# Attention and two MLPs on one core: the start of ScalarE, a later load and eight low halves moved

## The chip, the cores and the metric

The kernel runs on one core of a Trainium2 chip. A core has TensorE (PE: matrix products, with its weight loads PEld), VectorE (DVE), ScalarE (ACT), GpSimd (POOL) and SyncE (SP); SyncE and GpSimd issue the DMAs here, each from a queue that is worked off in order. The metric is the time on the device from the first to the last instruction, in microseconds; less is better.

## The reference

Four batches of 768 steps and eight heads of 48 go through an attention with complex decays, then through a block that mixes tokens and channels, then through a channel MLP behind a layer norm.

```python
def _attn_ref(q, k, v, a_re, a_im):
    mag = np.sqrt(a_re * a_re + a_im * a_im)
    scale = np.minimum(mag, 0.999) / (mag + 1e-06)
    a_re_n, a_im_n = (a_re * scale, a_im * scale)
    for t in range(S):
        ar, ai = (a_re_n[:, :, t, :, None], a_im_n[:, :, t, :, None])
        new_re = ar * S_re - ai * S_im
        new_im = ar * S_im + ai * S_re
        kv = np.einsum('bhd,bhe->bhde', k[:, :, t], v[:, :, t])
        S_re, S_im = (new_re + kv, new_im)
        y[:, :, t] = np.einsum('bhd,bhde->bhe', q[:, :, t], S_re)

def _moe_ref(x, w_tok1, w_tok2, w_ch1, w_ch2):
    h = np.maximum(x.transpose(0, 2, 1) @ w_tok1, 0.0) @ w_tok2
    u = x + h.transpose(0, 2, 1)
    return u + np.maximum(u @ w_ch1, 0.0) @ w_ch2

def _moe2_ref(x, g_ln, w_ch1, w_ch2):
    mu = np.mean(x, axis=-1, keepdims=True)
    var = np.mean((x - mu) ** 2, axis=-1, keepdims=True)
    xn = (x - mu) / np.sqrt(var + 1e-06) * g_ln
    return x + np.maximum(xn @ w_ch1, 0.0) @ w_ch2
```

## The kernel before

The recurrence is turned into matrix products over chunks of 128 steps: with the running product of the normalised decays at hand, the rows of q and k of a chunk are multiplied and divided by it (the corrections), and a head is then a handful of 32-bit matmuls. The decays of a batch come as three pieces of 128 rows, each in two halves of 384 columns. The program is written as four generators whose steps a driver records in turn, and a scheduler sets each engine's order from that recording:

- `gen_E` works on VectorE through a helper (all of its VectorE instructions have line L179). `gen_A` normalises a half piece: ScalarE squares (L228), takes a logarithm (L232), an exponential (L233) and a square with a running sum (L234), and VectorE joins them with four instructions of 384 columns and one of 768; then come the scan steps, each two products `p<-aj` and two sums `aj<-p`. `gen_L2` finishes the scan over blocks. `gen_C` applies the corrections to a half piece and stores it into the tiles of the heads by DMA, the part for k by L355 and the part for q and k by L356 (`stk`, or for the first batch's later heads tiles named `w`). For batch 0 the pieces 0 and 1 go first, then piece 2 (`PARTS`). `load_a` (L63) loads decays of a batch and a piece; `load_qk` (L151) loads q and k.
- `gen_P` does the heads on TensorE: transposes (L425), scores (L438), states (L465), output (L485, L497), with the mask (L443) and the state scan (L466) on VectorE, and the loads of v (L376) on SyncE.
- `gen_W` prepares the weights. A weight comes as raw 64-bit numbers (L513); VectorE unpacks it (L530, L531) to 32 bits, ScalarE rounds it, scaled, to 16 bits (L533, the high half), VectorE subtracts that from the scaled weight (L534, the low half). Weights 0 to 3 are those of the token layers, 4 to 15 those of the first channel MLP, 16 to 27 those of the second.
- `gen_M` does the MLPs with three 16-bit matmuls for each product (high times high, high times low, low times high: L566, L567, L568): the first token layer in two halves (`tok1_half`, result L608 and L610), the second (`tok2`, L612 to L627), the channel MLP (`mlp`, hidden layer by L574 on ScalarE and L576 on VectorE), and the layer norm (`gen_LN`, column sums by 32-bit matmuls L680 and L699 with the constant `ones`).

TensorE accumulates in eight PSUM banks: two under the tag m1, three under m2, one each under sc, tr and y. The second accumulation of the first batch's MLP, which runs five steps behind the first, uses sc, tr and y. The first batch's pass is the one in which everything is prepared; the three batches after it run with all weights in place, and the heads of a later batch are recorded among the MLP steps of the batch ahead.

## Time and profile before

| | us |
|---|---|
| median of 3 runs (lowest to highest) | 973.39 (971.98 to 974.5) |
| the profiled execution, its own time | 972.28 |
| its span, first to last instruction | 970.6 |
| TensorE busy | 834.6 (86%) |
| VectorE busy | 744.1 (77%) |
| ScalarE busy | 496.8 (51%) |
| mean granted TensorE clock | 0.957 |

The busy times are sums over stages that differ: a share of 86% says nothing of the stage in which an engine waits. The rows that follow the change are read by stage. A row of a timeline gives start, length, engine, line, operation, destination and source, and in brackets how long the engine sat idle before it and what released it; where instructions overlap in the pipeline, the distance of two starts is the time that one holds its engine.

### The profile page before, as it was taken

To read this page: it belongs to the slowest core of one execution; us is meant where nothing else is said; L and a number is where in the kernel's file an instruction comes from. 1 tells how busy PE (TensorE), PEld (TensorE's weight loads), DVE (VectorE), ACT (ScalarE), POOL (GpSimd) and SP (SyncE) were. 2 spreads that over 40 slices of the span, in tenths; PEclk is the share of its full clock that TensorE was granted. 3 is DMA by queue.
4 is the path that set the end of the run, shared out by engine and by line. 5 is a ranking of instruction groups with operands and counts; after the bars stand their busy time and mean duration, and the time that the engine had idled before them with its cause. 6 is when DMAs were issued, how large, how long until landed. Compare 5 with 4: busy or idle time off the path is not lost.

```text
span 970.6 us, 15833 instructions
## 1 busy us (share of the span) xinstructions
PE 834.6 (86%) x5738; PEld 570.6 (59%) x5738; DVE 744.1 (77%) x1597; ACT 496.8 (51%) x1364; POOL 59.6 (6%) x113
## 2 busy tenths in 40 slices
PE   0018989699988899999889999799999999999996
PEld 0018979356556687655556666466666666656563
DVE  6999957999997788997979999988675523264543
ACT  6014434533543459434868972574676533354532
POOL 0000101000102100001010000011000000011110
PEclk9999975799999789999899999999999999999998
DMA  8024475421447533114245120343120102255572
GB/s 283 0 57 128 160 208 164 167 79 66 153 133 225 159 107 107 64 34 130 57 118 168 32 62 1 115 127 80 55 56 25 50 1 90 86 194 195 190 239 94
DMA packets 45287, 108.28 MB, mean 112 GB/s; under 512 B 5904, under 2 KB 28560, under 8 KB 45200
## 3 DMA queue, kind: packets, MB, share of 16 engines
q1 hardware_dynamic: 36816, 61.57, 21.5%
q0 software_dynamic: 8384, 45.62, 14.2%
q8 instruction: 47, 0.77, 0.3%
q14 instruction: 40, 0.33, 0.1%
HBM read 77.20 MB, written 11.01 MB: 91 GB/s over the span
## 4 chain that ended last, share of the span: by engine, by line
PE 40%; DVE 28%; DMA 11%; issue 10%; ACT 6%; SPq 4%; POOL 0%; DVEq 0%; POOLq 0%; ACTq 0%
PE m L566 11%; PE m L567 11%; PE m L568 11%; DVE t L179 6%; DVE aj L179 4%; DVE p L179 4%; DMA stk<-t 3%; DMA stk<-qk 2%; DMA raw<-in_wm 2%; DMA aj<-in_a 2%; DVE hid L576 2%; PE sc L438 2%; SPq L355 2%; SPq L356 1%; DVE qk L179 1%
## 5 line engine op out<-in xcount | busy, mean ns | idle before, releaser
L576 DVE SCALAR_TENSOR_TENSOR hid<-m,hid 128x384 f16<-128x384 f32 x198 | 109.4, 553 | 113.4 <-ACT hid L574 112.8
L566 PE MATMUL m<-u,w 128*128 128x384 f16 x576 | 189.6, 330 | 1.5 <-DVE u L626 1.3
L567 PE MATMUL m<-u,w 128*128 128x384 f16 x576 | 189.8, 330 | 0.0
L568 PE MATMUL m<-u,w 128*128 128x384 f16 x576 | 189.7, 329 | 0.0
L574 ACT ACTIVATE hid<-m 128x384 f16<-128x384 f32 x198 | 96.0, 485 | 180.8 <-PE m L568 179.7
L567 PE MATMUL m<-hid,w 128*128 128x384 f16 x540 | 177.3, 329 | 12.3 <-DVE hid L576 12.0
L568 PE MATMUL m<-hid,w 128*128 128x384 f16 x540 | 177.0, 328 | 0.0
L568 PEld LDWEIGHTS <-w 128*128 128x128 f16 x1176 | 116.5, 99 | 89.7 <-issue 20.8
L567 PEld LDWEIGHTS <-w 128*128 128x128 f16 x1176 | 116.9, 99 | 75.1 <-issue 6.5
L566 PEld LDWEIGHTS <-w 128*128 128x128 f16 x1176 | 116.7, 100 | 75.2 <-issue 7.6
L566 PE MATMUL m<-hid,w 128*128 128x384 f16 x540 | 129.6, 328 | 2.4 <-ACT hid L574 2.1
L425 PE MATMUL tr<-cst,stk 96*128 96x96 f32 x125 | 17.1, 260 | 77.8 <-DMA stk<-qk 75.0
L179 DVE SCALAR_TENSOR_TENSOR t<-t 128x384 f32<-128x384 f32 x120 | 64.8, 549 | 8.5 <-ACT t L228 5.7
L425 PEld LDWEIGHTS tr<-cst,stk 96*128 96x128 f32 x125 | 13.9, 151 | 81.4 <-issue 71.3
L179 DVE TENSOR_TENSOR p<-aj 128x288 f32<-128x288 f32 (+2 forms) x150 | 52.7, 392 | 0.8
L179 DVE TENSOR_TENSOR t<-aj,I 128x768 f32<-128x768 f32 x40 | 36.4, 953 | 16.5 <-DMA stk<-t 11.8
L438 PE MATMUL sc<-stk 96*128 96x128 f32 x300 | 46.2, 289 | 2.7 <-DVE xc L682 1.4
L438 PEld LDWEIGHTS sc<-stk 96*128 96x128 f32 x300 | 42.3, 202 | 5.8 <-DVE r L443 1.7
L533 ACT ACTIVATE w<-raw 128x768 f16<-128x768 f32 x28 | 25.4, 906 | 30.0 <-DVE raw L531 29.8
L513 POOL DMA_DIRECT2D raw<-in_wm x48 | 25.9, 540 | 238.3 <-DVE w L534 109.0
L574 ACT ACTIVATION_READ_ACCUMULATOR hid<-m 128x1 f32 x198 | 38.5, 194 | 0.0
L546 ACT ACTIVATE sq<-sq 128x768 f16<-128x768 uint8 x28 | 23.6, 843 | 27.8 <-DVE sq L545 27.8
(268 smaller groups left out, 1670.7 us busy)
## 6 DMA issues: line engine op xcount, KB each, us to landing
raw<-in_wm POOLq DMA_DIRECT2D x48, 768.0 KB, 4.6
qk<-in_qk SPq DMA_DIRECT2D x23, 384.0 KB, 4.7
aj<-in_a SPq DMA_DIRECT2D x9, 768.0 KB, 5.0
stk<-t SPq DMA_DIRECT2D x40, 144.6 KB, 3.3
stk<-qk SPq DMA_DIRECT2D x40, 144.6 KB, 3.1
raw<-in_wt SPq DMA_DIRECT2D x6, 768.0 KB, 5.4
v<-in_v SPq DMA_DIRECT2D x32, 144.0 KB, 2.2
x_d<-xc SPq DMA_DIRECT2D x24, 192.0 KB, 2.5
```

Of the source, the lines that this page charges most:

```text
L179: r = getattr(nc.vector, n)(*a, **k)
L355: nc.sync.dma_start(out=stk[b, h][d0:d0 + m, hf], in_=R[r:r + m])
L425: T.transpose(tr[:, c * 96:(c + 1) * 96], qc(c, 1), eye[0:96, 0:96])
L438: last = T.matmul(sc[:, (c % 3) * P:(c % 3 + 1) * P], qc(c, 1), qc(c, 0), start=True, stop=True)
L513: (nc.sync if n < NSY else nc.gpsimd).dma_start(out=raw.bitcast(U8), in_=w_src[n].bitcast(U8)[:, 3:3 + 8 * S])
L533: wact[n] = A.activation(out=dst[:, :, 0], in_=w, func=AF.Copy, scale=WS).ins
L546: A.activation(out=t[:, HB:2 * HB].bitcast(F16), in_=bad_, func=AF.Copy, accum_out=wstat[:, n:n + 1])
L566: T.matmul(out_, wh, xh_, start=first, stop=False)
L567: T.matmul(out_, wh, xl_, start=False, stop=False)
L568: T.matmul(out_, wl, xh_, start=False, stop=last)
L574: A.activation(out=hl[:, 0], in_=p, func=AF.Relu, accum_out=hstat[:, n_h[0]:n_h[0] + 1])
L576: last[:] = [V.scalar_tensor_tensor(out=hl[:, 1], in0=p, scalar=0.0, in1=hl[:, 0], op0=ALU.max, op1=ALU.subtract).ins]
```

## The change

It has four parts. ScalarE's first instruction on a half piece of batch 0 is held back until the sum of the half piece ahead is done, and the square of the layer norm's gains (`gstat`) goes from VectorE to ScalarE. The decays of batch 1 are loaded when all corrections of batch 0 are recorded, not each after its own piece. For the weights 4 to 11 the low half is formed by TensorE: the 32-bit weight times a scaled identity (`eye_w`) minus the high half times a 16-bit identity (`eye_m`), accumulated in the bank y, for each of its two halves of 384 columns, and ScalarE copies the result out. The first token layer's halves accumulate in tr instead of y, and heads with an even number take m1 instead of tr for the transposes.

```diff
--- before.py
+++ after.py
@@ -96,7 +96,6 @@
     V.memset(bias[:, 5:6], TINY)
     b_ln, b_one, b_eps, b_zero, b_eps_s, b_tiny = (bias[:, i:i + 1] for i in range(6))
     A.activation(out=eye_h, in_=eye, func=AF.Copy, scale=WS * WS)
-    V.tensor_tensor(out=gstat, in0=gl, in1=gl, op=ALU.mult)
 
     w1 = ap.tile([P, FT, 4 * DM], F16, name="w1")
     w1_f = w1.rearrange("p k s -> p (k s)").bitcast(F32)
@@ -210,9 +209,12 @@
                 for i in part:
                     for x in gen_C(b, i, Ct, st, nxt_q):
                         yield x
-                    if b + 1 < B:
+                    if b and b + 1 < B:
                         load_a(b + 1, i)
                     yield ("done", b, i)
+                if b == 0 and part[-1] == 2:
+                    for i in range(3):
+                        load_a(1, i)
 
     av = aj.rearrange("p x (j k r) -> p x j k r", j=6, k=KB)
 
@@ -225,14 +227,15 @@
                 ah = steps(aj, i, hf)
                 t = scratch(b, 2 * i + hf)
                 s4, s5, s6, s7 = (t[:, j * HB:(j + 1) * HB] for j in range(4))
-                A.activation(out=t[:, 0:2 * HB].rearrange("p (x h s) -> p x h s", x=2, h=2), in_=ah, func=AF.Square)
+                with (tc.issue_after(fin["ln"]) if b == 0 and "ln" in fin else ExitStack()):
+                    A.activation(out=t[:, 0:2 * HB].rearrange("p (x h s) -> p x h s", x=2, h=2), in_=ah, func=AF.Square)
                 yield "wait"
                 V.scalar_tensor_tensor(out=s4, in0=s4, scalar=TINY, in1=s5, op0=ALU.add, op1=ALU.add)
                 nn = s4
                 A.activation(out=s5, in_=nn, func=AF.Ln)
                 A.activation(out=s5, in_=s5, func=AF.Exp, scale=-0.5, bias=b_ln)
-                A.activation(out=s6, in_=s5, func=AF.Square, scale=1.0 / 0.4995,
-                             accum_out=rstat[:, 6 * b + 2 * i + hf:6 * b + 2 * i + hf + 1])
+                fin["ln"] = A.activation(out=s6, in_=s5, func=AF.Square, scale=1.0 / 0.4995,
+                                         accum_out=rstat[:, 6 * b + 2 * i + hf:6 * b + 2 * i + hf + 1]).ins
                 if b == 0:
                     V.tensor_scalar(out=s7, in0=s5, scalar1=-EPS / 0.4995, scalar2=1.0, op0=ALU.mult, op1=ALU.add)
                 else:
@@ -531,8 +534,21 @@
         V.scalar_tensor_tensor(out=y.bitcast(U32), in0=y.bitcast(U32), scalar=5, in1=pad[0], op0=ALU.logical_shift_right, op1=ALU.bitwise_or)
         w = y.bitcast(F32).rearrange("p (i s) -> p i s", i=2)
         wact[n] = A.activation(out=dst[:, :, 0], in_=w, func=AF.Copy, scale=WS).ins
+        if NW0 <= n < NW1:
+            if not eye_w:
+                eye_w.append(ap.tile([P, P], F32, name="eye_w"))
+                eye_w.append(ap.tile([P, P], F16, name="eye_m"))
+                A.activation(out=eye_w[0], in_=eye, func=AF.Copy, scale=WS)
+                A.activation(out=eye_w[1], in_=eye, func=AF.Copy, scale=-1.0)
+            for i in range(2):
+                p = psum("y", 1)[:, 0:HB]
+                T.matmul(p, eye_w[0], w[:, i], start=True, stop=False)
+                T.matmul(p, eye_w[1], dst[:, i, 0], start=False, stop=True)
+                A.activation(out=dst[:, i, 1], in_=p, func=AF.Copy)
+            return
         wop[n] = V.scalar_tensor_tensor(out=dst[:, :, 1], in0=w, scalar=WS, in1=dst[:, :, 0], op0=ALU.mult, op1=ALU.subtract).ins
 
+    eye_w = []
     again = {}
     last = []
 
@@ -599,7 +615,7 @@
     def tok1_half(g, r1):
 
         cs = slice(g * (DM // 2), (g + 1) * (DM // 2))
-        p = psum("y", 1)[:, 0:DM].rearrange("p (j s) -> p j s", j=2)
+        p = psum(TOK1T, 1)[:, 0:DM].rearrange("p (j s) -> p j s", j=2)
         for j in range(2):
             for tc_ in range(NCH):
                 n, k = divmod(2 * tc_ + j, 3)
@@ -714,6 +730,7 @@
     rs = {}
 
     def gen_M():
+        A.activation(out=gstat, in_=gl, func=AF.Square)
         r1 = [ap.tile([P, 2, DM], F16, tag="hid", name="hid", bufs=NHID) for _ in range(2)]
         tok1_half(0, r1)
         u = big()[:, 0:6 * HB].bitcast(F16).rearrange("p (x c s) -> p x c s", x=2, c=3)
@@ -1077,6 +1094,7 @@
 
 
 LATE = 1
+NW0, NW1, TOK1T = 4,12, "tr"
 PARTS, EB2 = ((0, 1), (2,)), 4000
 STG = 8
 NWH, NWB, NWE = 5, (7, 7), 0
@@ -1103,7 +1121,7 @@
 CD, VA = 3, 7
 PNA, PNC, EG, PNT = 0, 0, -1, "m1"
 SR, DH, VR = 1, 1, 0
-TGO, TGE, FILL, FK = ("m1", "sc", "m1", "m2"), ("sc", "m2", "tr", "m2"), 0, 0
+TGO, TGE, FILL, FK = ("m1", "sc", "m1", "m2"), ("sc", "m2", "m1", "m2"), 0, 0
 GC, WPE, SPE = 0, 0, 0
 YH = 32
 SR=1;GC=1;SPE=0;CD=2;LNPE=2;NKICK=0;NKT=1;K_TOK=12;YH=12;NDW=2;NHID=3;NST=3;NV=2;NSK=0;TGO=("m1","sc","m1","m2");PR=0.5;P0=-4;EB=3500;ET=2500;QH=16;WOFF=130;WSTEP=10;EB0=500;EB1=5000;KE=12;DH=1;IL=5;W0=4;NWARM=(0,0);NWB=(0,0);WG=4;WPE=0;EG=7;NWE=0;CGS=0;NS0=6;NSM=99;NSY=3
```

In the kernel after, the two matmuls of a pair are L545 and L546 and their copy is L547; lines of before stand 3 further down up to L425 and 16 to 18 further down behind the new ones (L425 is L428, L566 is L582, L228 is L231).

ScalarE at the start of the program, before: `t`, `u` and `w1` are the scratch tiles of the first half pieces.

```order
L228 ACTIVATE t_132<-aj_69 128x768
L228 ACTIVATE u_110<-aj_69 128x768
L232 ACTIVATE t_132<-t_132 128x384
L228 ACTIVATE t_230<-aj_69 128x768
L233 ACTIVATE t_132<-t_132,bias_84 128x384
L232 ACTIVATE u_110<-u_110 128x384
L228 ACTIVATE w1_106<-aj_69 128x768
L234 ACTIVATE t_132,rstat_88<-t_132 128x384
```

And in the kernel after:

```order
L231 ACTIVATE t_131<-aj_69 128x768
L235 ACTIVATE t_131<-t_131 128x384
L236 ACTIVATE t_131<-t_131,bias_84 128x384
L237 ACTIVATE t_131,rstat_88<-t_131 128x384
L231 ACTIVATE u_109<-aj_69 128x768
L235 ACTIVATE u_109<-u_109 128x384
L236 ACTIVATE u_109<-u_109,bias_84 128x384
L98 ACTIVATE eye_h_83<-cst_82 128x128
L733 ACTIVATE gstat_95<-gl_85 128x3
L541 ACTIVATE eye_w_1413<-cst_82 128x128
L542 ACTIVATE eye_m_1414<-cst_82 128x128
L237 ACTIVATE u_109,rstat_88<-u_109 128x384
```

The four squares of different half pieces that stood among each other's steps now come one half piece at a time, and four instructions that need the constants `cst` and `gl` stand ahead of the second half piece's sum.

SyncE among the first heads, before: the stores of the second half of piece 1, then a load of decays and four loads of v, then the stores of piece 2.

```order
L355 DMA w_648<-w_106 16x771
L356 DMA w_648<-qk_111 16x771
L63 DMA aj<-in_a 128x2x768
L376 DMA v<-in_v 128x288 x4
L355 DMA w_648<-w_106 32x771
L355 DMA w_1115<-w_106 48x771
```

After:

```order
L358 DMA w_646<-w_105 16x771
L359 DMA w_646<-qk_110 16x771
L379 DMA v<-in_v 128x288 x2
L63 DMA aj<-in_a 128x2x768 x2
L379 DMA v<-in_v 128x288
L358 DMA w_646<-w_105 32x771
L358 DMA w_1112<-w_105 48x771
```

Two of the loads of decays stand here now, where one stood; of the two others of before one was issued among the first pieces' stores, and the third of after comes behind the last stores of piece 2. One load of v fewer stands ahead of the stores.

TensorE at the second token layer before the first step of the channel MLP, before: `m` is a bank of m1, L623 the addition of x by an identity.

```order
L623 MATMUL m_1624<-eye_h,xh 128x128
L623 LDWEIGHTS xl
L623 MATMUL m_1624<-eye_h,xl 128x128
L566 LDWEIGHTS hid
L566 MATMUL m_1651<-w_106,hid 128x384
```

After, at the same place:

```order
L639 MATMUL m_1622<-eye_h,xh 128x128
L639 LDWEIGHTS xl
L639 MATMUL m_1622<-eye_h,xl 128x128
L545 MATMUL y<-raw,eye_w 128x384
L546 LDWEIGHTS eye_m
L546 MATMUL y<-w_105,eye_m 128x384
L545 MATMUL y<-raw,eye_w 128x384
L546 LDWEIGHTS eye_m
L546 MATMUL y<-w_105,eye_m 128x384
L582 LDWEIGHTS hid
L582 MATMUL m_1656<-w_105,hid 128x384
```

Two pairs stand here between two blocks of the token layer. Of the sixteen pairs one stands among the sixth to eighth head, six between there and the first step of the channel MLP, and nine among its steps; the matmuls of the second accumulation that go into y come behind the last pair.

## Rows read from the trace of the kernel before

**Rows 1.** Windows by stage: from:to, length, busy us (x instructions) per engine, clock, DMA

```profile
0.00:70.00 70.00, 0.20 (x2) 0.23 (x3) 58.70 (x189) 18.88 (x40) 2.02 (x13) 1.00 0.35 110
70.00:133.40 63.40, 53.88 (x281) 52.52 (x280) 54.73 (x147) 23.84 (x52) 4.00 (x10) 1.00 0.55 163
133.40:165.00 31.60, 31.16 (x161) 29.80 (x162) 18.82 (x31) 13.33 (x32) 2.16 (x4) 0.53 0.51 169
165.00:193.00 28.00, 19.21 (x117) 12.33 (x115) 26.17 (x50) 16.52 (x43) 3.77 (x7) 0.74 0.50 164
193.00:302.00 109.00, 102.20 (x618) 60.64 (x618) 107.39 (x209) 46.72 (x111) 10.32 (x19) 1.00 0.39 125
302.00:365.00 63.00, 55.72 (x363) 43.63 (x361) 49.02 (x84) 31.96 (x82) 5.31 (x7) 0.81 0.50 150
365.00:970.60 605.60, 572.27 (x4202) 371.46 (x4202) 429.30 (x891) 345.57 (x1006) 32.02 (x53) 0.99 0.31 95
```

**Rows 2.** Groups by line and form, 128 to 305 us: busy us, mean ns

```profile
L534 DVE SCALAR_TENSOR_TENSOR w<-raw,w 128x768 f16<-128x768 f32 x26 | 24.8, 954 | 0.1
...
L574 ACT ACTIVATE hid<-m 128x384 f16<-128x384 f32 x35 | 17.0, 486 | 35.7 <-PE m L568 35.7
```

**Rows 3.** Timeline of VectorE (DVE), 12 to 32 us: start us, length us, instruction

```profile
12.99 0.16 DVE L99 TENSOR_TENSOR gstat<-gl 128x3 f32<-128x3 f32 x1 [0.74 <-DMA gl<-in_g]
...
27.20 0.61 DVE L179 TENSOR_TENSOR p<-aj 128x192 f32<-128x192 f32 x2
27.73 0.55 DVE L179 SCALAR_TENSOR_TENSOR w<-w 128x384 f32<-128x384 f32 x1
28.20 0.95 DVE L179 TENSOR_TENSOR aj<-aj,w 128x768 f32<-128x768 f32 x1
29.07 0.41 DVE L179 TENSOR_TENSOR aj<-p 128x96 f32<-128x96 f32 x2
29.41 0.95 DVE L179 TENSOR_TENSOR aj<-aj,w 128x768 f32<-128x768 f32 x1
30.28 0.61 DVE L179 TENSOR_TENSOR p<-aj 128x192 f32<-128x192 f32 x2
...
31.39 0.63 DVE L179 TENSOR_TENSOR p<-aj 128x192 f32<-128x192 f32 x2
```

**Rows 4.** Timeline of TensorE (PE), waits of 0.9 us and more among the heads

```profile
93.81 0.71 PE L425 MATMUL tr<-cst,w 96*128 96x96 f32 x3 [3.54 <-DMA w<-qk]
...
128.74 0.24 PE L566 MATMUL y<-xh,w 128*128 128x192 f16 x1 [0.90 <-DVE hid L610]
...
133.46 0.44 PE L425 MATMUL m<-cst,w 96*128 96x96 f32 x3 [3.07 <-DMA w<-w]
```

**Rows 5.** Timeline of VectorE, the last product of the third piece

```profile
127.45 0.96 DVE L179 TENSOR_TENSOR u<-u,aj 128x768 f32<-128x768 f32 x1
```

**Rows 6.** Timeline of SyncE's DMA queue, four stores of one half piece

```profile
91.10 2.44 SPq L356 DMA_DIRECT2D w<-qk  x4
```

**Rows 7.** Timeline of TensorE, matmuls of the first token layer

```profile
124.91 0.37 PE L567 MATMUL y<-xl,w 128*128 128x192 f16 x1
125.07 0.37 PE L568 MATMUL y<-xh,w 128*128 128x192 f16 x1
...
128.82 0.24 PE L567 MATMUL y<-xl,w 128*128 128x192 f16 x1
```

**Rows 8.** Timeline of TensorE, two column sums and the matmul behind each

```profile
250.64 0.81 PE L680 MATMUL m<-r,cst 128*128 128x384 f32 x2
251.29 0.33 PE L567 MATMUL sc<-hid,w 128*128 128x384 f16 x1
...
315.24 1.32 PE L680 MATMUL sc<-r,cst 128*128 128x384 f32 x2
316.39 0.33 PE L568 MATMUL m<-hid,w 128*128 128x384 f16 x1
```

**Rows 9.** Timeline of TensorE, its longest wait between heads and channel MLP

```profile
175.97 0.34 PE L566 MATMUL m<-w,hid 128*128 128x384 f16 x1 [2.43 <-ACT hid L608]
```

## The prediction

> **What bounds the kernel now.** I read first the busy time of each engine by stage [rows 1]: seven windows of the span of 970.6 us, cut where the work changes. Up to 70 us TensorE has nothing to do; VectorE is busy for 58.7 us of it and sets the pace alone (normalising the decays and scanning them). From 70 to 133.4 the first heads share VectorE with the rest of the corrections: TensorE 53.9 of 63.4 us, VectorE 54.7, neither full. [...] From 165 to 193 VectorE leads (26.2 of 28), and TensorE has 8.8 us idle. From 193 to 302, the first channel MLP, VectorE is busy for 107.4 of 109 us and TensorE for 102.2: VectorE bounds, TensorE is 6.8 us behind it. From 302 to 365 neither is full. The remaining 605.6 us belong to TensorE (572.3), with VectorE at 429. No instruction of the change lies behind the first channel MLP, so whatever it is worth has to be earned or lost before 365 us, in 365 us where TensorE idles for about 102 us, 70 of them in the start.
>
> Then I read what ended TensorE's three long waits among the heads [rows 4]: 3.54 us at 93.8 for a DMA that brings corrected rows to the head tiles, 0.90 at 128.7 for VectorE, 3.07 at 133.5 for the DMA of the sixth head. Both DMAs follow the last correction product of their piece; the last one of all starts at 127.45 [rows 5].
>
> **Part 1, the start (ScalarE piece by piece, gstat on ScalarE).** VectorE's wait for gl disappears (0.74 us, with the 0.16 us of the product, [rows 3]). In exchange the second piece's reduction on ScalarE now stands behind eye_h, gstat, eye_w and eye_m, so it waits for the same gl until about 13 us. Following both orders with the durations of [rows 3] (0.47 us from one 384-wide instruction to the next, 0.87 for a 768-wide one), VectorE has got through the same amount of work at 17 us in both, but in another mixture: two pieces are finished instead of one. Scan steps therefore begin earlier and stand between instructions of later pieces. That pays, since a bare step takes 1.11 us (30.28 to 31.39) while a step with other work between its halves takes 0.53 + 0.34 = 0.87 [rows 3]. Five more steps are covered in the new order: 5 x 0.24 = **-1.2 us**; nothing, if ScalarE, which now does four instructions and a round trip to VectorE for one piece before it touches the next, holds VectorE up; so 0 to -1.5. I take -1.
>
> **Part 2, the second batch's decays loaded later.** Each of its half pieces costs VectorE four 384-wide instructions and one of 768: 4 x 0.47 + 0.87 = 2.75 us. Two of them stand among the first heads, ahead of the last corrections; in the new order they, and the ScalarE instructions with them, come behind. Counting VectorE's order of before and after with these durations, the products of the second piece of the first batch (the ones that feed the wait at 93.8) move ahead by 6.6 us, those of the third piece (127.45) by 4.1; the masks of two heads move back by 5. With part 1: the wait of 3.54 us goes, since its data comes 7.6 us earlier, and the last product starts at 127.45 - 4.1 - 1 = 122.3. From there to the sixth head's start lie 133.46 - 127.45 = 6.0 us of DMA issues and landings, which I keep: start at 128.3, **-5.1 us**. What could spoil it is SyncE's queue, which is in order: four issues of L356 take 2.44 us there [rows 6], and a load of q and k now stands between the L355 and the L356 of the second half of the first piece, a load of v between those of the second piece. A wait of one such group, 2.4 us, costs nothing while the corrections are 7 us ahead. The two loads of decays come ahead of the third piece's issues, where one stood before; they are issued as soon as SyncE is free, long before 120 us, so I cost them at nothing.
>
> What follows is full TensorE time [rows 1], so work that enters it counts in full. The second half of the first token matmul (18 matmuls) stood before the sixth head, at a spacing of 0.08 us [rows 4, 7]; in the new order it stands between the halves of the sixth head, where the 0.16 us of 124.91 to 125.07 is more likely [rows 7]: 18 x 0.16 = +2.9. One pair of part 3 lies here too, +1.5. So the head stage ends 5.1 - 2.9 - 1.5 = 0.7 us earlier; 3 if the DMAs land faster than before with less beside them, or the token matmul runs at the high clock. I take **-2**.
>
> **Part 3, eight low halves on TensorE and ScalarE.** Removed: eight subtractions of 0.95 us on VectorE [rows 2], 8 x 0.87 = 7.0 us. Added: sixteen pairs of a 32-bit and a 16-bit matmul, 128x384. The 32-bit one is in the trace, as a column sum of the same shape: it holds TensorE from 250.64 to 251.29, 0.65 us at the high clock, and from 315.24 to 316.39, 1.15 us, at the low one [rows 8]. The 16-bit one is two spacings of 192 columns: 0.16 or 0.32 [rows 4, 7]. So a pair is 0.81 or 1.47 us and sixteen are 13.0 to 23.5. ScalarE gets sixteen copies like the 0.49 us ones of the hidden layer [rows 2], 7.8 us; in the window from 193 to 302 it is busy for only 46.7 of 109 us [rows 1], so I cost them at nothing, at most the wait named among the rivals.
>
> By the new order one pair falls into the heads (counted above), six between the heads and the first step of the MLP, nine among its steps. The six meet a stretch where TensorE waits for VectorE or ScalarE (2.43 us at 176.0, [rows 9], and 8.8 in all): 6 x 0.81 to 6 x 1.47 = 4.9 to 8.8 fit, just. VectorE, which leads there, has by my count 20.5 us of work from the last head's evacuation to the end of the second token matmul instead of 23.5: **-3 us**.
>
> In the MLP stretch VectorE falls to 107.4 - 4 = 103.4 us, and TensorE rises to 102.2 + 9 x 0.81 = 109.5 against 109 now. So **the bound passes from VectorE to TensorE, and the stretch cannot get shorter**: +0.5 if every wait of TensorE is filled, more by every one that stays. I take **+1**. This is where 7 us of VectorE work go without a gain. From 302 to 365 VectorE's last 4 us less and TensorE's 7.3 us idle let me take **-1**. The other changes (three PSUM tags exchanged) I cost at nothing: the bank that the halves use, y, is wanted by the second accumulation of the MLP, whose matmuls are moved behind the last pair, and these are the same matmuls later.
>
> [...]
>
> **Sum.** -2 (start and heads) - 3 + 1 - 1 = -5 us on the profiled execution of 972.28 us, which is 967.3. The median of the runs, 973.39, is 1.1 above it: **968.4 us**.
>
> **The rivals.**
> (a) Slower: the pairs cost TensorE more than their time. In a pair the 16-bit matmul needs ScalarE's high half, which comes behind VectorE's unpacking, and TensorE's queue is in order, so the MLP stands still meanwhile. For it: TensorE would be the bound there, 109.5 us of work in 109. Against it: raw weights are unpacked several steps ahead. With 1 us lost at each of nine pairs and the gain of the heads at its lower end (-1, -2): 973.4 + 9 + 0.5 - 3 = 980. It turns the result slower from 0.5 us a pair on (4.5 us + 0.5 against 5).
> (b) The heads swallow their gain: the third window is full TensorE at the low clock, with 2.9 + 1.5 = 4.4 us more in it, and the six pairs at 1.47 us fill all of the idle time behind it. Then only the start's 1 us and the last 1 remain, against +1: 972.4, no change to be told.
> (c) More than I say: the clock. The window of 133.4 to 165 is full of 32-bit matmuls and granted 0.53; the token matmul of 128.7 runs at twice the rate of the one at 124.9 after the first wait in a long while [rows 4, 7]. If the 16-bit matmuls that now stand between the sixth head's halves and inside the later heads bring the high clock with them, up to a third of the 31.2 us goes: 968.4 - 8 = 960. Against it: the heads before have two token blocks among them as well, and stay low.
> [...]
> (d) The low halves do nothing for VectorE, since something else that it waits for sets the pace; but at 107.4 of 109 us busy there is no room for that, and I give it no chance of its own.
>
> **How the numbers follow.** A difference under 0.3%, 2.9 us, can't be told from none. My forecast (-3 to -8) has 0.45, (c) 0.13, (b) 0.20, (a) 0.22. Faster 0.57 (the forecast's own cases nearly all, and (c)), same 0.21, slower 0.22. The likeliest case's own range is 965 to 970.5. For 8 in 10 it must take in (b), most of (c) (960, less 1 for the start at its upper end, 2 for DMAs that land sooner) and (a) up to 0.6 us a pair, 978.
>
> **What would show it.** The scan's end a microsecond sooner; no DMA wait of 3 us at the third head; the sixth head at about 128; first hidden layer at about 188; TensorE's busy share from there to 302 at 97% or more with VectorE's under it. Wrong: waits of TensorE for ScalarE's w in front of L546, a sixth head that starts where it did, or a third window with another granted clock.

## The result: 948.1 us, 26 us less than before, and the profile after

The changed kernel takes 948.12 us (median of 4 runs, 947.54 to 951.91) where the kernel before, beside it on the same chip, takes 973.94 (4 runs, 971.98 to 975.13). The ratio is 0.9745, interval 0.9714 to 0.9776. Its profiled execution took 947.54 us with a span of 945.4, which is 24.7 us less than the profiled execution of before; the stage times below add up to that difference. The forecast was 968.4, range 957 to 978: right in sign, five times too small in size, and outside its range.

The windows below are cut at the same events in both kernels: first head, end of the first batch's heads (its last row of residuals xl), last result of that batch's second token layer, first result of the second batch's second token layer, end. Columns as in [rows 1]. First the kernel before:

```profile
69.80:165.20 95.40, 85.44 (x443) 82.60 (x444) 73.78 (x179) 37.37 (x85) 6.16 (x14) 0.84 0.53 164
165.20:190.70 25.50, 16.90 (x104) 11.09 (x103) 23.84 (x46) 16.04 (x41) 3.23 (x6) 0.72 0.53 177
190.70:410.90 220.20, 203.99 (x1344) 136.84 (x1344) 202.55 (x399) 110.95 (x288) 16.71 (x28) 0.95 0.39 122
410.90:970.60 559.70, 528.31 (x3851) 340.05 (x3848) 385.46 (x790) 313.59 (x914) 31.48 (x52) 0.99 0.31 96
```

And the kernel after:

```profile
67.60:155.70 88.10, 80.17 (x456) 75.45 (x456) 77.44 (x185) 40.09 (x89) 7.78 (x17) 0.90 0.64 195
155.70:177.30 21.60, 17.10 (x109) 10.52 (x110) 21.00 (x50) 15.14 (x43) 1.62 (x3) 0.92 0.40 139
177.30:386.70 209.40, 199.27 (x1375) 133.95 (x1374) 195.32 (x383) 113.85 (x297) 20.20 (x28) 1.00 0.41 129
386.70:945.40 558.70, 530.12 (x3850) 341.77 (x3848) 384.94 (x789) 314.25 (x914) 28.23 (x52) 0.98 0.32 96
```

The first head starts 2.2 us sooner, the heads are 7.3 us shorter, the stretch to the MLP 3.9, the MLP stretch (first batch's channel MLP with the second batch's heads) 10.8; behind 411 and 387 us the two agree within 1 us. So the whole gain is made before 387 us. In the MLP stretch TensorE has 31 matmul records more (27 of them of the pairs) and is still busy 4.7 us less, at a mean granted clock of 1.00 instead of 0.95; its waits (length less busy) fall from 16.2 to 10.1 us.

What answers to [rows 1] at the old cuts: the third window is granted 0.68 instead of 0.53, and in the fifth VectorE is busy for 96% instead of 99% of the time.

```profile
133.40:165.00 31.60, 27.00 (x143) 21.51 (x142) 29.22 (x57) 20.76 (x50) 4.31 (x8) 0.68 0.63 222
165.00:193.00 28.00, 26.40 (x169) 16.00 (x167) 27.47 (x56) 16.47 (x39) 2.16 (x4) 1.00 0.34 113
193.00:302.00 109.00, 103.83 (x651) 65.68 (x650) 104.53 (x193) 52.14 (x127) 15.49 (x21) 1.00 0.48 153
```

VectorE's timeline after, start and length: the first scan step starts at 16.31 (before 22.24), the run of bare steps starts at 34.74 instead of 30.28 and has 7 steps instead of 13, and the scan's end, the copy to `I`, stands at 42.61; the last product of the third piece, [rows 5], starts at 122.67.

```profile
16.31 0.62 DVE L178 TENSOR_TENSOR p<-aj 128x192 f32<-128x192 f32 x2
...
34.74 0.63 DVE L178 TENSOR_TENSOR p<-aj 128x192 f32<-128x192 f32 x2
...
42.61 0.26 DVE L178 COPY I<-aj 128x192 f32<-128x192 f32 x1
...
122.67 0.95 DVE L178 TENSOR_TENSOR u<-u,aj 128x768 f32<-128x768 f32 x1
```

Before, the first step and the same copy:

```profile
22.24 0.61 DVE L179 TENSOR_TENSOR p<-aj 128x192 f32<-128x192 f32 x2
...
44.85 0.26 DVE L179 COPY I<-aj 128x192 f32<-128x192 f32 x1
```

TensorE's timeline after, with its waits in brackets, answers to [rows 4, 7, 9]. The wait of 3.54 us at the third head is 1.00 us; the sixth head starts at 124.83, right behind the fifth head's matmuls, without a wait; the 18 matmuls of the first token layer's second half run from 125.79 to 127.28, 0.08 us each, the high clock's pace; some pairs wait for ScalarE's copy of a pair before (L547), 4.3 us in all; the first MLP matmul runs at 176.09 (before 188.58).

```profile
87.01 0.69 PE L428 MATMUL m<-cst,w 96*128 96x96 f32 x3
88.69 0.58 PE L428 MATMUL m<-cst,w 96*128 96x96 f32 x2 [1.00 <-DMA w<-qk]
124.83 0.43 PE L428 MATMUL m<-cst,w 96*128 96x96 f32 x3
125.79 0.25 PE L582 MATMUL tr<-xh,w 128*128 128x192 f16 x1
125.88 0.24 PE L583 MATMUL tr<-xl,w 128*128 128x192 f16 x1
161.10 1.65 PE L545 MATMUL y<-raw,eye_w 128*128 128x384 f32 x2 [2.49 <-ACT w L547]
171.14 0.94 PE L545 MATMUL y<-raw,eye_w 128*128 128x384 f32 x2 [0.94 <-ACT w L547]
176.09 0.32 PE L582 MATMUL m<-u,w 128*128 128x384 f16 x1 [0.34 <-DVE u L642]
```

The store into the sixth head's tile of the rows of q and k from the first half of piece 2, with the us from issue to landing at the end of the line, before (124 to 133.5 us) and then after (119 to 126.8):

```profile
w<-qk SPq DMA_DIRECT2D x1, 96.4 KB, 6.2
```

```profile
w<-qk SPq DMA_DIRECT2D x1, 96.4 KB, 2.5
```

And the groups by line and form after, for [rows 2, 8]: the sixteen pairs cost TensorE 15.1 + 5.4 us of busy time where they stand, partly at the low clock (the median of one 32-bit pass is 500 ns, so 32 x 0.055 = 1.8 us of it is slowness).

```profile
L545 PE MATMUL y<-raw,eye_w 128*128 128x384 f32 x32 | 15.1, 555 | 4.3 <-ACT w L547 4.3
L546 PE MATMUL y<-w,eye_m 128*128 128x384 f16 x16 | 5.4, 337 | 0.1
```

**Where the clock shows.** I read the clock from the lengths of 32-bit weight loads and not from the granted record, on the figures of the last section. In the heads of batch 0, groups by form, before (67 to 165 us) and then after (67 to 156):

```profile
L497 PEld LDWEIGHTS m<-U,w 96*128 96x128 f32 x60 | 16.2, 332 | 0.9 <-DVE U L466 0.9
```

```profile
L500 PEld LDWEIGHTS m<-U,w 96*128 96x128 f32 x60 | 13.2, 269 | 1.8 <-DVE U L469 1.4 <-DVE t L178 0.3
```

In the heads of batch 1, before (298 to 399) and then after (264 to 374):

```profile
L497 PEld LDWEIGHTS y<-U,stk 96*128 96x128 f32 x80 | 14.5, 222 | 0.8 <-DVE U L466 0.3 <-issue 0.2
L485 PEld LDWEIGHTS y<-v,sT 128*128 128x128 f32 x48 | 9.1, 241 | 0.9 <-ACT junk L395 0.7 <-DVE r L697 0.2
```

```profile
L500 PEld LDWEIGHTS y<-U,stk 96*128 96x128 f32 x80 | 12.4, 190 | 0.7 <-DVE U L469 0.3
L488 PEld LDWEIGHTS y<-v,sT 128*128 128x128 f32 x48 | 7.1, 191 | 1.4 <-ACT junk L398 1.3
```

One load of 128 columns takes about 332 ns in some stretches and 190 in others, and 16-bit matmuls of 384 columns start 0.32 and 0.16 us apart (before, from 313.32 and from 249.83 us). I take both for the clock and call the two the low and the high one; that is my reading of these lengths. I add up, over a stretch, what each 32-bit load takes beyond 0.192 us (0.165 with 96 columns; L465 takes 164 ns behind 410 us of before), and for each 16-bit matmul at the slow pace 0.42 ns a column, which is (0.32 - 0.16) / 384: **the clock's loss**. It is a reckoning from lengths, not a record of the profile. From the first head to the end of the MLP stretch it falls from 69.3 us (heads 51.1, stretch 5.1, MLP 13.1) to 41.1 (39.8, 1.2, 0.1). The 13.1 us of the MLP stretch before all lie between 302 and 365 us, the window granted 0.81 in [rows 1]; in the window from 193 to 302 there is none. Waits in the same span fall from 34.8 to 22.6 (length less busy of the first three windows above). With the pairs, +13.0 (16 x 0.81) and +1.8, that makes -28.2 - 12.2 + 14.8 = -25.6 us; measured are 319.1 - 341.1 = -22. Some 4 us of this sum do not close.

The same stretch cut once more, where as much TensorE work is done in both kernels (pairs left out, each matmul counted at its spacing at the high clock): at 302 us before and at 293.9 after. Before:

```profile
190.70:302.00 111.30, 104.31 (x630) 61.80 (x630) 109.69 (x214) 47.00 (x113) 10.86 (x20) 1.00 0.38 123
302.00:410.90 108.90, 99.68 (x716) 75.04 (x715) 92.86 (x186) 63.95 (x175) 5.85 (x8) 0.89 0.40 122
```

And after:

```profile
177.30:293.90 116.60, 111.43 (x683) 68.76 (x682) 114.62 (x216) 59.27 (x142) 16.57 (x23) 1.00 0.44 142
293.90:386.70 92.80, 87.84 (x694) 65.19 (x693) 80.71 (x168) 54.57 (x157) 3.63 (x5) 1.00 0.39 112
```

The first part gets 5.3 us longer and the second 16.1 us shorter. VectorE is busy for 98% of the first part after, TensorE for 96%.

### The profile page after: what moved, and what is told of

Read it like the earlier page. It is cut to its first block, busy times and chain, and to the rows that moved or that the text cites. A ratio compares the mean times of both kernels' runs of the same rounds, so it can differ in the third digit from the quotient of the medians.

```text
span 945.4 us, 15969 instructions
## 1 busy us (share of the span) xinstructions
PE 826.7 (87%) x5786; PEld 561.7 (59%) x5786; DVE 736.4 (78%) x1588; ACT 504.5 (53%) x1383; POOL 59.8 (6%) x113
## 4 chain that ended last, share of the span: by engine, by line
PE 42%; DVE 32%; DMA 10%; issue 7%; ACT 6%; SPq 3%; POOL 0%; DVEq 0%; ACTq 0%; POOLq 0%
PE m L583 12%; PE m L582 11%; PE m L584 11%; DVE t L178 6%; DVE aj L178 5%; DVE p L178 4%; DVE hid L592 3%; DMA stk<-t 2%; DMA aj<-in_a 2%; DMA stk<-qk 2%; PE sc L441 2%; DVE pad L533 1%; DMA raw<-in_wm 1%; DVE qk L178 1%; DVE w L549 1%
## 5 line engine op out<-in xcount | busy, mean ns | idle before, releaser
L582 PE MATMUL m<-u,w 128*128 128x384 f16 x576 | 188.9, 328 | 1.9 <-DVE u L642 1.2
L582 PEld LDWEIGHTS <-w 128*128 128x128 f16 x1176 | 115.6, 99 | 74.0 <-issue 6.3
L582 PE MATMUL m<-hid,w 128*128 128x384 f16 x540 | 127.6, 326 | 1.6 <-ACT hid L590 1.3
L428 PE MATMUL m<-cst,stk 96*128 96x96 f32 x10 | 2.5, 377 | 71.1 <-DMA stk<-qk 71.1
L428 PEld LDWEIGHTS m<-cst,stk 96*128 96x128 f32 x10 | 1.8, 231 | 71.4 <-issue 67.5
```

Of the source, the lines that this page charges most:

```text
L582: T.matmul(out_, wh, xh_, start=first, stop=False)
```

## The experiments

Each run stands beside runs of the kernel before on the same chip (medians 971.8 to 974.1). A is the start, B the later load, C the pairs with the exchanged tags. "MLP stretch" is the third window, with TensorE's waits and the clock's loss in it; "heads end" is the end of the first batch's heads. Stage times are of each profiled execution.

| kernel | median us | ratio (interval) | heads end | MLP stretch, waits, loss | loss in heads |
|---|---|---|---|---|---|
| before | 973.94 | 1 | 165.2 | 220.2, 16.2, 13.1 | 51.1 |
| only_start (A) | 971.47 | 0.9993 (0.9977-1.0009) | 162.3 | 222.0, 18.3, 12.7 | 52.2 |
| only_late (B) | 971.99 | 0.9989 (0.9963-1.0014) | 151.7 | 243.5, 22.8, 35.2 | 35.2 |
| only_pairs (C) | 958.82 | 0.9854 (0.9831-0.9877) | 162.8 | 218.4, 9.1, 11.2 | 40.8 |
| dve_low_tags (A+B) | 959.23 | 0.9853 (0.9822-0.9884) | 154.5 | 229.3, 22.4, 16.0 | 35.7 |
| early_load (A+C) | 964.22 | 0.9913 (0.9881-0.9945) | 172.6 | 215.7, 13.0, 4.0 | 47.8 |
| no_start (B+C) | 960.44 | 0.9860 (0.9829-0.9890) | 164.1 | 217.1, 11.9, 5.2 | 44.9 |
| after (A+B+C) | 948.12 | 0.9745 (0.9714-0.9776) | 155.7 | 209.4, 10.1, 0.1 | 39.8 |

**One part undone.** The start:

```diff
-                with (tc.issue_after(fin["ln"]) if b == 0 and "ln" in fin else ExitStack()):
-        A.activation(out=gstat, in_=gl, func=AF.Square)
+    V.tensor_tensor(out=gstat, in0=gl, in1=gl, op=ALU.mult)
```

> The kernel after, with the start as before: no holding back of ScalarE's first square, the product gstat on VectorE again. Theory (three gains that add up: the start, the late load of decays, the low halves): the scan ends 2.2 us later than in the kernel after and the delay reaches the end, so 948.1 + 2.2 = 950.3. Rival (the clock: the gain comes from 16-bit matmuls among the heads, whatever the start does): also about 948 to 950, so this run alone prices the start and decides nothing else. If the scheduler's new order is what counts, and not the part, it may come out anywhere between 946 and 960.

The load:

```diff
-                    if b and b + 1 < B:
+                    if b + 1 < B:
-                if b == 0 and part[-1] == 2:
-                    for i in range(3):
-                        load_a(1, i)
```

> The kernel after, with the loads of the second batch's decays issued each behind its own piece, as before. Theory (three gains): the two half pieces come back among the first heads (5.5 us of VectorE work), the third and the sixth head start later by about 7 us, and the time is 954 to 956. Rival (clock): the heads are full TensorE time whatever feeds them, and the pairs and token matmuls among them still hold the clock; then no more than the 3.5 us wait of the third head comes back: 948 to 951.5.

The low halves back on VectorE, once with the new PSUM tags and once with those of before (that is A+B):

```diff
-NW0, NW1, TOK1T = 4,12, "tr"
+NW0, NW1, TOK1T = 0,0, "tr"
```

> The kernel after, with all low halves on VectorE again (no pairs on TensorE), the PSUM tags left as after. Theory: VectorE's 7 us come back in the first channel MLP, where it bounds, and the stretch from the first MLP step to the second token layer of batch 1 is 209 + 10 = 219 us again: 955 to 959. Rival (clock): without the pairs the heads and the stretch from 285 to 385 us fall back to the low clock (granted 0.5 to 0.8): 960 or more, with TensorE's busy time up although it does 13 us less. Second rival (pairs hardly matter, the gain is of the order of the heads): 948 to 951.

```diff
-NW0, NW1, TOK1T = 4,12, "tr"
+NW0, NW1, TOK1T = 0,0, "y"
-TGE = ("sc", "m2", "m1", "m2")
+TGE = ("sc", "m2", "tr", "m2")
```

> As the run with all low halves on VectorE, and the PSUM tags of the first token layer (y) and of the even heads (tr) as before too. Theory: the tags cost nothing, so the same time as with the tags left, 955 to 959, within 1 us. Rival (the tags decide: with tr taken by the token layer and m1 by the heads the order of the heads changes): 3 us or more above or below the run with the tags left.

Undoing one part costs 12 (start), 16 (load) or 11 us (pairs with their tags); 2, 6 to 8 and 7 to 11 had been expected, so for the start and the load the forecast missed. dve_low, expected at 955 to 959, takes 974.52 us (1.0031, 1.0008 to 1.0054): without pairs, the tags alone cost 15 us against dve_low_tags. They are a part of C and not worth nothing by themselves.

**One part alone.** The two edits of the others undone together:

```diff
 only_start:  load early again; NW0, NW1, TOK1T = 0,0, "y"; old TGE
 only_late:   start as before;  NW0, NW1, TOK1T = 0,0, "y"; old TGE
 only_pairs:  load early again; start as before
```

> The kernel before with the first part alone (ScalarE piece by piece, gstat on ScalarE). Undoing one part of the kernel after cost 12 (start), 16 (late load) and 11 us (low halves), 39 in sum where the whole change gives 25. Theory (the parts complete each other: the late load moves VectorE work from the heads into the channel MLP, which VectorE bounds, and the low halves make room for it there): the start alone brings its 2.2 us at the end of the scan and little more, 969 to 972 beside 972 to 974 of before. Rival (the parts add, each with the price of its removal): 972 - 12 = 960.

> The kernel before with the late load of the second batch's decays alone. Theory (the parts complete each other): the third head starts 7 to 9 us earlier and the first MLP step too, but the stretch from the first MLP step to the second token layer of batch 1, 220 us before, is 226 or more, as VectorE bounds it and has 5.5 us more to do there: 968 to 974 in all. Rival (the parts add): 972 - 16 = 956.

> The kernel before with the low halves on TensorE and ScalarE and the new PSUM tags alone. Theory (the parts complete each other): the heads are as before (sixth head at 133, end at 165), the stretch from the first MLP step to the second token layer of batch 1 is shorter by 3 to 6 of 220 us: 966 to 970. Rival (the parts add): 972 - 11 = 961 or less. Rival (clock): the pairs among the heads raise the granted clock from 0.5 to 0.7 between 133 and 165 and from 0.88 to 0.98 behind 307: 8 to 12 us less, 960 to 964.

The start alone is worth nothing, the load alone nothing, the pairs alone 14 to 15 us, all together 25: the parts do not add up. (The pairs alone were expected at 966 to 970 and came out within the range of the rival that the parts add, 961 or less; the start and the load alone missed that rival by 11 and 16 us.) B alone is the instructive one. Its heads end 13.5 us earlier than before, and its MLP stretch is 23 us longer, 22 of them the clock's loss. Windows of only_late, first and second half of that stretch:

```profile
170.70:285.50 114.80, 105.36 (x619) 61.55 (x619) 110.84 (x219) 47.45 (x112) 11.41 (x20) 0.97 0.34 114
285.50:414.20 128.70, 115.31 (x725) 90.27 (x724) 101.73 (x202) 63.91 (x176) 5.73 (x9) 0.77 0.39 113
```

In the first half VectorE is busy 97% of the time: what no longer stands before 170 us stands here. In the second the second batch's heads run at a granted clock of 0.77, and their weight loads (groups by form, 285 to 415 us of only_late) take 276 and 332 ns instead of 190:

```profile
L442 PEld LDWEIGHTS sc<-stk 96*128 96x128 f32 x96 | 18.6, 276 | 0.4 <-issue 0.2
...
L489 PEld LDWEIGHTS y<-v,sT 128*128 128x128 f32 x48 | 12.7, 332 | 3.9 <-ACT junk L399 3.7 <-issue 0.2
```

Counted in the trace, 279 16-bit matmuls stand there among the heads' 344 records of 32-bit ones (324 before, 469 after; 72 are the heads' own each time, the rest the MLP's), and the longest time from one 16-bit matmul's start to the next one's is 30.1 us (11.7 before, 4.3 after).

**No work for low halves at all.** The eight low halves are written as zeros by ScalarE, so the low halves of these weights are left out and neither VectorE nor TensorE forms them (A and B kept):

```diff
-                T.matmul(p, eye_w[0], w[:, i], start=True, stop=False)
-                T.matmul(p, eye_w[1], dst[:, i, 0], start=False, stop=True)
-                A.activation(out=dst[:, i, 1], in_=p, func=AF.Copy)
+                A.activation(out=dst[:, i, 1], in_=w[:, i], func=AF.Copy, scale=0.0)
```

> The kernel after, but the low halves of the eight weights are zeros that ScalarE writes (sixteen copies scaled by 0): the pairs on TensorE and the subtractions on VectorE are both left out, so the output lacks these low halves. Theory (the gain of the part is VectorE's relief, and the pairs cost TensorE their time): 13 us less on TensorE, of which up to 7 lie in the bounded stretch: 941 to 948, with the granted clock behind 280 us at 0.97 or more as in the kernel after. Rival (clock: the pairs, 32-bit and 16-bit matmuls in otherwise idle moments, hold the clock up): without them it falls to 0.85 there, and the time is 952 or more.

953.12 us (0.9809, 0.9770 to 0.9847), within the rival's 952 or more, MLP stretch 218.6 with a loss of 9.4. This run keeps the new tags, so its neighbour without the relief is dve_low (974.52): freeing VectorE of the subtractions, with the order that the scheduler then finds, is worth 21 us there, and 6 us against A+B with the old tags. With the pairs' TensorE work on top it is 5 us faster still. Less work is slower than more: time is not a sum of work here.

**The exchanged tags.** Pairs with both tags of before, and with the token layer's alone exchanged:

```diff
 old_tags:  NW0, NW1, TOK1T = 4,12, "y";   TGE = ("sc", "m2", "tr", "m2")
 tr_heads:  NW0, NW1, TOK1T = 4,12, "tr";  TGE = ("sc", "m2", "tr", "m2")
```

> The kernel after with the two PSUM tags as before: the first token layer accumulates in y, the bank of the pairs, and even heads take tr for their transposes. Theory (the tags only matter without pairs, where the order of heads came out badly): the pairs and the token layer now wait for one bank, by 1 to 3 us before the first MLP step, 949 to 952. Rival (the tags decide, as the runs without pairs said: 974 with the new ones, 959 with the old): with the old ones 940 or less, or above 960.

> The kernel after with the even heads' transposes in tr again, as before, and the first token layer in tr as after. In the run with both tags as before the heads ended at 153.9 us instead of 155.7 and lost 4 us less to the low clock, but the stretch up to the first MLP step took 42 us instead of 22, with pairs and token layer in one bank. Theory (that bank was the fault, the heads' order the gain): 944 to 948. Rival (tr held by the heads delays the token layer, as it comes after them): 950 to 958.

old_tags takes 956.02 us (0.9828, 0.9794 to 0.9862), tr_heads 949.77 (0.9778, 0.9731 to 0.9826). With one bank for pairs and token layer the stretch between heads and MLP is 41.9 us instead of 21.6. TensorE's timeline of old_tags there:

```profile
169.43 1.62 PE L545 MATMUL y<-raw,eye_w 128*128 128x384 f32 x2 [7.08 <-DVE raw L534]
171.95 1.65 PE L545 MATMUL y<-raw,eye_w 128*128 128x384 f32 x2 [0.58 <-ACT w L547]
...
179.75 0.32 PE L582 MATMUL y<-xh,w 128*128 128x192 f16 x1 [0.61 <-ACT w L547]
```

A token matmul (L582) waits for a pair's copy. Eight pairs now stand ahead of this block of the token layer; the longest wait among them, 7.08 us, is for VectorE's unpacking of the next weight (L534), and the waits for a copy are 0.58 to 1.09 us each. The heads' tag makes 1.7 us by the medians, which is inside the interval. The one bank shows in the waits for a copy, about 5 us of the 20; the longest wait is one of order.

**One pair of weights fewer**, 4 to 10 instead of 4 to 11:

```diff
-NW0, NW1, TOK1T = 4,12, "tr"
+NW0, NW1, TOK1T = 4,11, "tr"
```

> The kernel after with seven low halves instead of eight on TensorE and ScalarE (weights 4 to 10). Theory (each low half off VectorE is worth its 0.9 us and a share of the clock): 1 to 2 us more than the kernel after, 949 to 951. Rival (what counts is the order into which the scheduler happens to fall, and a small change of its input moves the time by 10 us): more than 4 us away from 948, on either side.

954.89 us (0.9824, 0.9789 to 0.9860): one low half fewer costs 6.8 us. An eighth of the gain of C over A+B (11 us) would be 1.4. So a scheduled kernel can move by several microseconds with a small edit, and a part's price can't be read from one such step. The next runs therefore keep the order: the list of instructions is edited after it has been scheduled.

**Order kept: more VectorE work.** After's instructions with a copy of each pad step of weights 4 to 11, to a tile that nobody reads, ahead of the original:

```diff
+L535 SCALAR_TENSOR_TENSOR again_<-raw 128x768 uint8   (x8, VectorE)
 L535 SCALAR_TENSOR_TENSOR pad<-raw 128x768 uint8
```

> The kernel after with every engine's order kept instruction for instruction, but the first unpacking step of each of the eight weights done twice by VectorE, once into a tile that nobody reads: 8 x 0.92 = 7.4 us of VectorE put back at the places where its relief was. Theory (VectorE's work in the channel MLP sets the pace there, and what TensorE waits for brings the low clock): 7 us and up to 11 us of clock come back, 955 to 966, with the granted clock behind 280 us below 0.95. Rival (the gain is the order, TensorE is the bound now and VectorE has room): 948 to 950.

956.97 us (0.9842, 0.9790 to 0.9894), +8.9 us. The group of the added steps:

```profile
L535 DVE SCALAR_TENSOR_TENSOR again__96<-raw 128x768 uint8<-128x768 uint8 x8 | 7.6, 953 | 0.0
```

7.6 us of VectorE work cost about their length, while the clock's loss in the MLP stretch stays at 0.1. By the profiled executions it is +7.3: 3.0 in the heads for two of the copies (where the loss rises from 39.8 to 43.4), 1.9 up to the MLP for three and 2.1 in the MLP stretch for three. So in this order most of the VectorE time added before about 190 us counts.

**Order kept: less TensorE work.** The pairs' 32-bit matmul cut to 8 columns; the low half that results is a changed number:

```diff
-L545 MATMUL y<-raw,eye_w 128x384 f32, start
-L546 MATMUL y<-w,eye_m 128x384 f16, stop
+L545 MATMUL y<-raw,eye_w 128x8 f32, start, stop
+L546 MATMUL y<-w,eye_m 128x384 f16, start, stop
```

> The kernel after with every engine's order kept, but the 32-bit matmul of each of the sixteen pairs cut to 8 columns and the 16-bit one left alone, so the low halves of eight weights are wrong by the weight itself: 16 x 0.5 to 0.65 = 8 to 10 us less on TensorE, about 6 of it in the MLP. Theory (the pairs cost TensorE their time where it bounds): 940 to 945. Rival (the pairs fill waits, or hold the clock up): 948 or more, in the second case with a clock below 0.95 behind 280 us.

952.74 us (0.9780, 0.9742 to 0.9819). About 10 us of TensorE work (16 x 0.65) are gone, and nothing is gained. TensorE's waits in the MLP stretch go from 10.1 to 15.9 us and the loss from 0.1 to 3.6. So the pairs' TensorE time is not what sets the length of this stretch. Window of after_cut:

```profile
179.20:394.40 215.20, 199.23 (x1375) 134.72 (x1383) 195.95 (x383) 113.11 (x297) 20.25 (x28) 0.98 0.40 125
```

**Order kept: less VectorE work without pairs.** In the kernel before, and in A+B, the eight subtractions become 16-bit copies (changed low halves):

```diff
-L534 SCALAR_TENSOR_TENSOR w<-raw,w 128x768 f16<-f32   (954 ns)
+L534 COPY w<-w 128x768 f16<-f16                       (about 360 ns)
```

> The kernel before with every engine's order kept, but the eight subtractions of the low halves of weights 4 to 11 replaced by 16-bit copies of the high half on VectorE, so these low halves are wrong: a copy should take 0.25 to 0.5 us instead of 0.87, 3 to 5 us less on VectorE. Theory (VectorE's work sets the pace of the channel MLP): 3 to 5 us and part of the 11 us of low clock go: 960 to 969. Rival (without another order the relief is lost in other waits): 971 to 973.

> The run with the start and the late load but no pairs and the old tags (959.2 us), its order kept, with the same eight copies in place of subtractions (low halves wrong). Theory (VectorE's relief is what the pairs bring): 948 to 955, with fewer waits of TensorE in the MLP. Rival (the order): 958 to 960.

The changed numbers lead the program's own range test to its general path, so these two took 13,917 and 13,908 us; their stages up to the start of the last ordinary output are read, which lies at 963.3 us before, 961.8 in before_cut, 952.8 in dve_low_tags, 950.9 in ab_cut. 4.7 us of VectorE work less gain 1.5 and 1.9 us, and the loss in the MLP stretch stays (13.1 and 11.2; 16.0 and 16.9). The 16-bit matmuls among the second batch's heads are as many as in the kernel with the same order (324 in before and before_cut, 315 in both of A+B). So in these two orders the VectorE relief alone does not bring back the clock.

**The clock by added 16-bit matmuls.** Into B alone go 64 dummy matmuls among the second batch's heads, and with after's order kept 46 (behind every fourth head matmul) or 93 (every second) among the first batch's:

```diff
 late_fill (on only_late):
+                if H <= n < 2 * H:
+                    y = y or ps_(3)
+                    warm(4, y, last)
 mix4, mix2 (on after, order kept):
+LDWEIGHTS eye_m
+MATMUL y<-cst,eye_m 128x384 f16    (behind each 4th, each 2nd)
```

> The run with the late load alone (972 us), plus 64 matmuls that compute nothing that is used: four 16-bit ones of 384 columns behind the scores of each half of the eight heads of the second batch, 64 x 0.16 = 10 us of TensorE time at the high clock. Theory (in that run TensorE loses about 27 us between 290 and 370 to the low clock, because 32-bit head matmuls stand there alone): the granted clock of that stretch rises from 0.5 to 0.9 or more and the time falls, by 27 - 10 at best, to 955 to 965. Rival (the low clock only goes with a TensorE that VectorE and the DMAs keep waiting, and time is set by those): 972 to 982, with the clock up or not.

> The kernel after with every engine's order kept, plus one 16-bit matmul of 384 columns that computes nothing used (its bank is free then) behind every fourth 32-bit matmul of the first eight heads, 46 in all: 7.4 us of TensorE at the high clock, 14.7 at the low one. [...]

> The same with a 16-bit matmul behind every second 32-bit one, 93 in all: 15 us of TensorE at the high clock, 30 at the low one. Theory (16-bit matmuls among 32-bit ones bring the high clock): still more weight loads at 0.19 us, but twice the added work: 938 to 950. Rival (the added matmuls cost their time): 960 to 978.

late_fill: 967.54 us (0.9947, 0.9918 to 0.9975), 4.5 us under only_late, where 7 to 17 had been expected; the loss in the MLP stretch falls from 35.2 to 20.3, the dummies cost 64 x 0.16 = 10 us themselves, and TensorE's waits rise from 22.8 to 25.6 (its profiled execution, 974.18, is among its longest). mix4: 949.78 us (0.9758, 0.9726 to 0.9790), loss in the heads 39.8 to 31.6. mix2: 953.67 (0.9798, 0.9771 to 0.9824), loss 22.9. The weight loads of the heads, 67 to 156 us, of mix4 and then of mix2, with the added matmuls, follow:

```profile
L500 PEld LDWEIGHTS m<-U,w 96*128 96x128 f32 x60 | 10.8, 224 | 2.1 <-DVE U L469 2.1
```

```profile
L500 PEld LDWEIGHTS m<-U,w 96*128 96x128 f32 x60 | 9.2, 192 | 0.8 <-DVE U L469 0.5
...
L546 PE MATMUL y<-cst,eye_m 128*128 128x384 f16 x93 | 36.3, 390 | 0.0
```

From after to mix4 to mix2 the mean load falls from 269 to 224 and 192 ns: more of the heads run at the high clock when 16-bit matmuls stand among them, as rival (c) had it. It does not come with the first of them: they begin at 79.4 us in mix4 and 78.4 in mix2, and the first weight load of 96x128 at the high clock's length stands at 116.3 us, behind 22 dummies, and at 104.4, behind 27. What let the clock rise there these runs do not show. Among these heads the dummies cost TensorE as much as they return or more: by the distance to the next start the 93 of mix2 hold it for about 20 us (0.16 to 0.33 us each, waits left out), where the loss falls by 16.9, and the 46 of mix4, at 0.16 to 0.32 us, cost 7.4 to 14.7 for 8.2. Whether useful 16-bit work in their place would pay was not tried. No version has a median under that of the kernel after.

## Why the prediction was wrong

**Right.** The end of the start: -1 forecast for the scan, -2.2 measured, with six more steps covered where five were forecast. The wait of 3.54 us at the third head goes (1.00 is left). The last product: 122.3 forecast, 122.67 measured. The stretch between heads and MLP: -3 forecast, -3.9 measured, with VectorE busy for 21.0 of 21.6 us; TensorE's loss at the low clock fell there by 3.9 as well (5.1 to 1.2), which the prediction did not count. TensorE does wait for L547 there (0.94 us between the two pairs in a row, and once 2.49). In front of L546 it waits 0.1 us in all, so rival (a) did not come. Nothing lies behind the MLP. One sign does not follow from the prediction's own sum: before, the first hidden layer stands at 190.24, and -5 gives 185, not 188; it came at 177.75.

**The heads' term was mis-sized: -2 with the start, measured -9.5** (165.2 to 155.7, -7.3 without the start). The sixth head was put 5.1 us earlier and starts 8.6 earlier: the 6.0 us behind the last product, "which I keep", are 124.83 - 122.67 = 2.2. That entry took the wrong product, too. The head's first matmuls read the first half of its columns, which the product at 125.60 (after: 120.69) completes; the last product feeds the second half. And the store of that first half took 6.2 us to land before and 2.5 after. From the sixth head on, +4.4 was put for new work in a stretch at the low clock, and the stretch is 0.9 us shorter: the token layer's 18 matmuls took 1.5 us and not 2.9, and the clock's loss from the sixth head to the end of the heads fell from 19.0 to 9.7 us. The prediction took that clock as it was; rival (c) named it, at 0.13, with up to 8 us.

**The step that failed is the MLP's: "the bound passes from VectorE to TensorE, and the stretch cannot get shorter", with +1 to 302 us and -1 from 302 to 365.** Together the stretch is 10.8 us shorter, and neither term holds. To the cut at 302 us before and 293.9 after, the bound did not pass: VectorE is busy for 114.62 of 116.6 us, TensorE for 111.43. The subtractions are gone there, but more of the second batch's corrections stand there (8 products `t<-aj,I` instead of 6, 4 `t<-qk,aj` instead of 2), ahead of heads that start at 264.8 instead of 298.3; the prediction counted only what leaves. This part is longer, +5.3 where +1 was put. The gain is all in the second part, -16.1 where -1 was put: the window of 302 to 365, granted 0.81 in [rows 1], was taken at its own pace, and 13.1 us of its TensorE time were loss at the low clock. After has 0.1. The waits of that part fall by 4.3 us as well (9.2 to 5.0), and -13.0 - 4.3 = -17.3 is near the measured -16.1. So TensorE's busy time there was a length at a clock, and the new order changed the clock.

**What made that clock was not the pairs themselves.** Rival (c) expected the 16-bit matmuls of the new order to bring it; among the first batch's heads mix4 and mix2 run longer at the high clock with such matmuls, though not from the first of them on. In the MLP stretch no run gives it to one instruction: after_cut leaves the pairs' 32-bit work out and loses 3.6 us, not 13; ab_cut and before_cut relieve VectorE and keep their loss; zero_low relieves it with a new order, and has 9.4. What goes with the loss over the kernels is the place of the second batch's heads in the order: they run from 264.8 us with 469 16-bit matmuls among them in after, from 298.3 with 324 in before. The kernels with 420 and more of these (after, old_tags, seven, tr_heads, no_start, early_load) have a loss of 0.1 to 6.5 us, those with 330 and fewer 11 to 35. only_pairs breaks the rule of thumb with 460 and 11.2; it has a stretch of 11.7 us without a 16-bit matmul. zero_low lies between, 402 and 9.4. It is a correlation over orders and shows no cause. late_fill, the one run that adds such matmuls there, lowers the loss by 15 us and pays 10 of them for the matmuls.

**The parts hang together.** B alone clears the heads and hands VectorE work to the MLP stretch, which gets 23 us longer, nearly all of it loss at the low clock; C takes VectorE work out of that stretch and fills TensorE's waits. The whole gain is there only with all three parts: B with C but without the start has 960.4. The prediction added terms for three parts, each at the other parts' old state; -13.6 for C, 0 for B and 0 for A do not make -25.

**Open.** Why the scheduler puts the second batch's heads so early with all three parts, and less with any two; what about that order keeps the clock high; how much of the 25 us is this one order's luck (seven weights instead of eight cost 6.8 us, so several microseconds of each verdict on a part are of that kind); and some 4 us that the account of waits, loss and pairs doesn't close. An order of before with only its head matmuls moved was not tried.

## What to carry to other kernels

Before an engine's busy time is used as a bound, look in each window for the loss at the low clock and take it out: the lengths of one form of instruction, at their shortest and as they stand in the window, showed it here (weight loads of 190 and 332 ns). The new order gave it all back here, 13.1 us. Count what comes into a window as well as what leaves it. Where a scheduler sets the order, parts do not add, so forecast the order of the whole change, and tell a part's price by runs that keep the order. Of relief on one engine ask which stage it lands in, since what clears one stage may fill the next.

## What the hardware showed that was not expected

In the kernel before TensorE stays at the low clock while it is busy with small 32-bit matmuls: in the third window of [rows 1], granted 0.53, where it is busy for 31.16 of 31.6 us, with loads of 332 to 333 ns in L485 and L497 against 190 in the later heads; and in the first heads, where no 16-bit matmul stands between them for 55.0 us (69.80 to 124.77), the loads are as long (the x60 group above holds both places). Being busy nearly all the time did not bring the high clock there.

The granted clock of a window did not always say so. [rows 1] has 1.00 for 70 to 133.4 us, where the loads are as long as in the third window (L497 `m<-U,w`: 332 and 333 ns). The window of before_cut in the place where [rows 1] has 0.53 for before:

```profile
133.46:164.70 31.24, 31.24 (x159) 30.23 (x158) 18.92 (x31) 13.06 (x31) 2.13 (x4) 1.00 0.50 166
```

And its weight loads of one form in the same stretch:

```profile
L497 PEld LDWEIGHTS m<-U,w 96*128 96x128 f32 x30 | 8.2, 333 | 0.0
```

The record says 1.00 and these 30 loads are at the low clock's 333 ns. So I go by the lengths of instructions here; the windows' 1.00 and 0.95 above are read together with them.
